# A new order for all engines in the last five rows of an attention and adapter kernel

## The chip, the core and the metric

The kernel runs on one core of a Trainium2 chip. The metric is the time of one execution in device microseconds. Three runs of the kernel before gave 99.35, 99.8 and 100.41 us; the median is 99.8 us. One more execution was profiled, and its trace is what is read below.

## What is computed

Eight batches ("rows" in the kernel, r = 0 to 7) of eight heads, 576 positions, head size 64. Heads 0 to 3 attend to the last 32 positions; heads 4 to 7 to every fourth of the last 128, so that after sorting the positions into four classes they are windowed attention too. Then every token goes through a router over eight small adapters.

```python
scores = scale * np.matmul(q, k.transpose(0, 1, 3, 2))
mask_plain = (rel >= 0) & (rel < window)
mask_dil = (rel >= 0) & (rel < window * dilation) & (rel % dilation == 0)
attn = softmax(where(mask, scores, -1e9));  x = attn @ v     # per head, then heads side by side
...
logits = x @ w_gate                          # 8 adapters, the best two are kept
z = x[mask] @ A[e]                           # 512 -> 16
delta[mask] += w[mask, k, None] * (z @ B[e]) # 16 -> 512, weighted by a softmax over the two
return x + delta
```

## The kernel before

One row's inputs are 3.5 MB of f32, which the loads turn into bf16 on their way into one of four input slots; one row's output is 1.2 MB of f32. Each row has two groups of four heads, g = 0 (plain) and g = 1 (dilated). The work of a row is a list of named steps, and each name is a letter, a row and a group or part:

- `L` loads, issued by POOL (lines 282, 314, 325). Row 4's are `L4a`, `L4b` (queries and keys of the two groups) and `Lw4` (values); rows 5 and 6 likewise. Row 7's are eight pieces, `Lq7..` for queries and keys and `Lv7..` for values. POOL runs them in its own order between its other work, and one waits at the head of POOL's queue until what it depends on is done.
- `S0rg`, `S1rg`: scores of the first five and the last four key blocks on PE, 24 and 20 matmuls (line 222, names `con,one` or `one` for the mask and `in` for the scores). `E0rg`, `E1rg`: their exponentials on ACT (line 370).
- `Vrg`: values, 26 matmuls (`in,p`). `Rrg`, `Nrg`: reciprocal and normalisation on DVE (lines 406, 409).
- `Brg`: cast to bf16 on POOL (line 416). `Trg`, `Ur`: 8 and 2 transposes on PE (lines 433, 457). `Crg`, `Cdr`, `Cpr`: their copies out of PSUM on ACT (lines 443, 446, 463, 467); in row 7 `Bx7` (ACT, line 418), `C71` (ACT, line 449) and `Cx7` (DVE, line 450) take a part.
- `Z0r`, `Z1r`: logits and adapter inputs, 20 matmuls (`aw,xt`); `Y0r`, `Y1r` their copies (ACT, line 491). `m0`, `m1`, `s12`, `top`, `tt`, `g2` on DVE and `th` on ACT (lines 503 to 513): the two best logits and their weights. `gzr`: the weighted adapter inputs on POOL (line 518; on DVE in row 7, as `gz7` and `gy7`).
- `Gr` (and `H7`): 5 transposes (line 523); `gcr`, `gnr` their copies on ACT (lines 539, 542). `Dr0` to `Dr2`: the adapters' outputs on PE (`bt,gc` or `bt,gn`). `Ar0` to `Ar2`: they are added to the row, on DVE (lines 570, 600) or, for parts of rows 4 to 7, by an ACT copy (`dx`, `dy`; lines 596, 576) and a POOL addition (lines 598, 578).
- `Or`: stores, issued by SP (lines 611, 615). Rows 0 to 4 are stored whole, at most two of these in flight; rows 5 to 7 in two halves. All stores wait for row 7's queries and keys to land (`late`).

Nothing schedules at run time. A text, `PLAN`, gives one order of all steps; each engine runs its own steps in that order, and what a step needs from another engine becomes a semaphore wait. A number behind `@` is the first PSUM bank of eight that a step's result gets; the step then also waits until all users of what stood in these banks before are done. So the order and the banks decide together who waits for whom. The text is all that differs between the two kernels.

Of the kernel before, what the change touches and what calls it, by code (L numbers as in the profile page):

```python
# [628 lines left out]
A00 S121@6 E121 S120@3 S021@1 Z01@0 E021 Z11@5 Y01 m01 Y11 m11 s121  # L629
S020@1 D02@0 V21@5 E120 top1 tt1 th1 g21 E020 A02 V20@0 R21 N21 R20 L4a  # L630
gz1 L4b G1@5 gn1 S130@6 N20 gc1 B21 E130 S031@3 D12@2 E031 S030@0 D10@5
T21@7 E030 C21 A12 S131@3 B20 Lw4 V30@0 L5a A10 E131 U2@7 T20@6 R30 N30
Cp2 B30 L5b V31@3 Cd2 C20 Z02@7 Y02 Z12@1 R31 N31 B31 T30@2 D11@6 Y12
C30 S041@4 A11 E041 S141@2 Lw5 S140@6 m02 E141 S040@0 m12 s122 tt2 U3@5
Cp3 th2 E040 top2 Cd3 g22 gz2 L6a V41@2 T31@0 E140 C31 V40@5 R41 N41
Z03@2 G2@0 Y03 gn2 Z13@1 L6b gc2 R40 Y13 N40 B40 Lw6 S051@2 D20@4 E051
A20 m13 S151@6 E151 S050@0 S150@2 E150 m03 s123 V51@5 top3 tt3 T40@3 th3
E050 C40 B41 g23 T41@4 C41 R51 V50@0 N51 R50 D22@5 N50 U4@7 gz3 Lq710
Lq711 Cd4 Cp4 G3@6 gn3 D21@3 gc3 A22 A21 Z04@7 Y04 B50 Lq700 Lq701
S060@0 D32@2 Z14@7 S161@5 m04 E060 Y14 m14 E161 s124 S160@0 A32 T50@7  # L640
E160 D30@3 S061@5 top4 V60@0 A30 tt4 R60 C50 E061 B51 Lv710 Lv711 Lv700
Lv701 O1 T51@3 N60 C51 V61@4 th4 g24 R61 N61 U5@7 S171@2 Cp5 Cd5 S070@0
Z05@7 E171 E070 Z15@6 Y05 S170@2 S071@4 Y15 m05 m15 top5 B60 gz4 E170
E071 s125 G4@0 B61 D31@6 tt5 th5 gn4 V70@1 T60@4 A31 gc4 V71@5 U6@0 C60
O0 g25 O2 gz5 G5@4 Cp6 Cd6 R70 N70 B70 T61@2 D41@0 D42@3 R71 N71 gn5 A41
C61 dx4 gc5 B71 Bx7 D40@5 Z06@2 Y06 Z16@4 Y16 A40 m06 A42 D52@3 m16 s126
dx5 top6 U7@7 Cp7 Cd7 tt6 T71@1 Cx7 C71 T70@4 D51@5 A52 th6 g26 A51
D50@0 A50 C70 gz6 Z07@2 Z17 m07 m17 s127 tt7 dy5 G6@5 gc6 O3 D61@0 th7
gn6 D62@7 A53 top7 O4 O51 O50 dx6 g27 D60@5 gy7 gz7 A62 dy6 A61 A63 O61
G7@3 H7 gm7 gn7 gc7 D72@0 dx7 A72 D71@1 A60 D73@6 O60 A71 D70@7 O71 A70  # L650
dy7 A73 O70
"""

_INS = ["qkv", "aw", "bt", "con"]
# [64 lines left out]
```

## Time and profile before

| | |
|---|---|
| median of three runs | 99.8 us (99.35 to 100.41) |
| the profiled execution | 100.24 us, of which the trace spans 98.5 us |
| granted TensorE clock | 0.983 (0.80 in the last stretch, from 90 us on, where PE has little to do) |
| busy: PE matmuls, ACT, DVE, POOL | 80.6, 71.1, 61.3, 55.5 us |
| loads on POOL's DMA queue | 14.23 MB, as they land |
| stores on SP's DMA queue and three small loads | 9.77 MB |

Times in the trace count from the first instruction. The span ends with the landing of the last store; 1.74 us of the profiled execution lie outside of it. A line of a step that a helper records shows the helper's line (222 for nearly all of PE), so steps are told apart by their operands and their place in the order.

### The profile page before, as it was taken

Reading aid. Unit: us, or ns where it says so; the run is one execution under the profiler, and the core shown is the slowest. Engines: PE = TensorE matmul, PEld = TensorE weight load, DVE = VectorE, ACT = ScalarE, POOL = GpSimd, SP = SyncE. Lnnn points to the kernel's source line nnn. Section 1 sums busy time; section 2 is a strip of 40 time slices with the busy share of each in tenths; the row PEclk is TensorE's granted clock in tenths of the full one; section 3 lists DMA queues with packets and bytes.
Section 4 is the critical chain, followed back from the end, with each engine's and each line's share of the span. In section 5 each row is a group of like instructions: output and inputs, shape, how many; then the busy total and the mean of one; then the engine's idle time right before and its main releaser. Section 6 shows DMA issues by size and latency. Waiting matters only on the chain.

```text
span 98.5 us, 3614 instructions
## 1 busy us (share of the span) xinstructions
PE 80.6 (82%) x1585; PEld 59.6 (60%) x1585; DVE 61.3 (62%) x138; ACT 71.1 (72%) x123; POOL 55.5 (56%) x76
## 2 busy tenths in 40 slices
PE   3999969959569989899899989997995989776500
PEld 2443457548356767689677768885883878564300
DVE  5770007706467179559737667976854999979810
ACT  5294494399938983996986889999596889957400
POOL 5999900810544058826574499397292464665820
PEclk9999999999999999999999999999999999999985
DMA  1999999999999999999999999999999999996894
GB/s 42 305 193 194 199 218 216 213 214 214 212 213 213 212 212 210 217 206 201 208 213 212 216 210 212 199 214 203 194 320 412 400 412 423 396 378 268 354 421 185
DMA packets 5999, 24.50 MB, mean 249 GB/s; under 512 B 864, under 2 KB 992, under 8 KB 5344
## 3 DMA queue, kind: packets, MB, share of 16 engines
q0 software_dynamic: 3968, 14.23, 73.2%
q1 hardware_dynamic: 1872, 9.77, 24.3%
q10 hardware_dynamic: 144, 0.28, 0.8%
q8 instruction: 12, 0.20, 0.7%
q14 instruction: 3, 0.02, 0.1%
HBM read 29.07 MB, written 9.44 MB: 391 GB/s over the span
## 4 chain that ended last, share of the span: by engine, by line
PE 56%; ACT 22%; DVE 9%; issue 4%; POOL 3%; POOLq 0%
PE ps L222 49%; ACT p L370 12%; PE ps L433 5%; DVE x L570 4%; DVE x L409 3%; ACT xt L443 2%; ACT gn L542 2%; PE ps L523 2%; ACT zs L491 1%; POOL x L578 1%; ACT gc L539 1%; ACT in L272 1%; POOL xb L416 1%; PE ps L457 1%; ACT xt L446 1%
## 5 line engine op out<-in xcount | busy, mean ns | idle before, releaser
L370 ACT ACTIVATE p<-ps 128x960 bf16<-128x960 f32 (+1 forms) x32 | 27.7, 902 | 4.3 <-PE ps L222 4.2
L416 POOL CAST xb<-x 128x1152 bf16<-128x1152 f32 (+1 forms) x16 | 18.2, 1139 | 16.9 <-DVE x L409 16.8
L222 PE MATMUL ps<-in,p 128*64 128x130 bf16 (+1 forms) x416 | 21.5, 221 | 3.9 <-ACT p L370 3.1
L409 DVE TENSOR_TENSOR x<-ps,rec 128x1152 f32<-128x1152 f32 x16 | 21.7, 1358 | 0.5
L222 PEld LDWEIGHTS ps<-in,p 128*64 128x64 bf16 (+1 forms) x416 | 17.1, 104 | 7.4 <-ACT p L370 4.2
L570 DVE TENSOR_TENSOR x<-x,ps 128x1024 f32<-128x1024 f32 (+1 forms) x16 | 17.5, 1117 | 4.6 <-PE ps L222 4.6
L406 DVE RECIPROCAL rec<-ps 128x18 f32<-128x18 f32 x16 | 4.3, 270 | 17.3 <-PE ps L222 17.1
L222 PEld LDWEIGHTS ps<-in 64*64 64x64 bf16 x576 | 10.8, 106 | 3.7 <-issue 1.9
L222 PE MATMUL ps<-in 64*64 64x96 bf16 (+1 forms) x576 | 11.8, 201 | 1.5 <-issue 1.5
L222 PE MATMUL ps<-warm 128*128 128x512 f32 x20 | 11.8, 737 | 1.5 <-DVE warm L226 1.5
L518 POOL TENSOR_TENSOR gz<-zs,g 128x640 bf16<-128x640 f32 x7 | 8.9, 1274 | 6.3 <-DVE g L513 6.3
L282 POOL DMA_DIRECT2D in<-in_qkv_dram x22 | 11.6, 572 | 1.4 <-POOLq L702 0.8
L222 PE MATMUL ps<-aw,xt 128*128 128x136 bf16 x160 | 11.2, 223 | 0.1
L443 ACT COPY xt<-ps 128x1024 bf16<-128x1024 bf16 x8 | 8.1, 1011 | 3.7 <-PE ps L433 3.6
L314 POOL DMA_DIRECT2D in<-in_qkv_dram x8 | 5.2, 648 | 9.2 <-PE ps L222 7.3
L222 PEld LDWEIGHTS ps<-aw,xt 128*128 128x128 bf16 x160 | 9.6, 98 | 0.9 <-ACT xt L443 0.4
L433 PE MATMUL ps<-one,xb 128*128 128x128 bf16 x128 | 9.6, 219 | 0.1
L222 PE MATMUL ps<-bt,gn 128*128 128x256 bf16 (+1 forms) x48 | 6.8, 263 | 2.0 <-ACT gn L542 0.8
L433 PEld LDWEIGHTS ps<-one,xb 128*128 128x128 bf16 x128 | 7.5, 98 | 1.5 <-POOL xb L416 0.7
L222 PEld LDWEIGHTS ps<-warm 128*128 128x128 f32 x20 | 4.5, 238 | 6.4 <-issue 4.9
L446 ACT COPY xt<-ps 128x1024 bf16<-128x1024 bf16 x7 | 7.3, 1038 | 1.0 <-PE ps L433 1.0
L222 PE MATMUL ps<-bt,gc 128*128 128x256 bf16 (+1 forms) x48 | 6.6, 255 | 1.5 <-ACT gc L539 1.5
(55 smaller groups left out, 102.4 us busy)
## 6 DMA issues: line engine op xcount, KB each, us to landing
out_dram<-x SPq DMA_DIRECT2D x5, 1152.0 KB, 5.7
in<-in_qkv_dram POOLq DMA_DIRECT2D x6, 576.0 KB, 7.6
out_dram<-x SPq DMA_DIRECT2D x6, 576.0 KB, 3.2
in<-in_qkv_dram POOLq DMA_DIRECT2D x10, 292.5 KB, 7.6
in<-in_qkv_dram POOLq DMA_DIRECT2D x10, 288.0 KB, 6.6
in<-in_qkv_dram POOLq DMA_DIRECT2D x2, 1152.0 KB, 23.3
in<-in_qkv_dram POOLq DMA_DIRECT2D x10, 146.2 KB, 8.0
in<-in_qkv_dram POOLq DMA_DIRECT2D x2, 434.2 KB, 13.8
```

The costliest lines, as they stand in the source:

```text
L222: return nc.tensor.matmul(o, lhsT=lhsT, rhs=rhs, start=start, stop=stop, skip_group_check=True)
L282: nc.gpsimd.dma_start(out=IN[r % SLOTS][half(a), at : at + n], in_=qkv[r, a, :, at - 2 * VB * a : at - 2 * VB * a + n],)
L314: return lambda: [nc.gpsimd.dma_start(out=IN[r % SLOTS][:, 2 * VB + QK * n : 2 * VB + QK * (n + m)].rearrange("p (j n) -> p j n", j=m), in ...
L370: return [nc.scalar.activation(p[:, :, :].rearrange("p h (s c) -> p h s c", c=PER)[:, :, b0 : b0 + nb, 0:SEG], PS[:, k.at : k.at + 2, 0 : ...
L406: rc = add(f"R{tag}", "DVE", ("el", 60), lambda: [nc.vector.reciprocal(rec[:, :].rearrange("p (b i) -> p b i", b=3), PS[:, k.at : k.at + 3 ...
L409: nm = add(f"N{tag}", "DVE", ("el", XG), lambda: [nc.vector.tensor_tensor(X[r][:, XG * g : XG * g + XG].rearrange("p (b i n) -> p b i n", ...
L416: add(f"B{tag}", "POOL", ("el", cut), lambda: [nc.gpsimd.tensor_copy(XB[r % 2][:, g, 0:cut], X[r][:, XG * g : XG * g + cut])], [nm] + free)
L433: nc.tensor.transpose(tp[j][:, 128 * u : 128 * u + 128], xb[:, g, 256 * u + 128 * j : 256 * u + 128 * j + 128], ident())
L443: return [nc.scalar.copy(xt[:, 0:2, 0:S].rearrange("p j (c i) -> p j c i", c=C)[:, :, :, 0:128], tp.rearrange("p j (i c) -> p j c i", c=C))]
L446: return [nc.scalar.copy(xt[:, 2:4, 0:512], tp)]
L518: return [en.tensor_tensor(GZ[i][:, us[0] : us[0] + n, :].rearrange("p u (e r) -> p u e r", e=E), zv()[:, us[0] : us[0] + n, 0:ER].rearran ...
L570: return [nc.vector.tensor_tensor(v, v, PS[:, k.at : k.at + nk].rearrange("p b n -> p (b n)"), ALU.add)]
```

## The change

The second half of `PLAN` is replaced, from `V30`'s successors to the end; the steps, their instructions, their sizes and their data are the same, and so is the first half of the order. All engines' orders and the bank numbers change in rows 3 to 7. The loads keep their order among themselves; the step names between which they stand change. A line or two of the text:

```diff
-T21@7 E030 C21 A12 S131@3 B20 Lw4 V30@0 L5a A10 E131 U2@7 T20@6 R30 N30
-Cp2 B30 L5b V31@3 Cd2 C20 Z02@7 Y02 Z12@1 R31 N31 B31 T30@2 D11@6 Y12
...
+T21@7 E030 C21 A12 S131@3 B20 Lw4 V30@0 E131 A10 U2@6 R30 N30 Cp2 L5a
+Cd2 T20@7 C20 V31@3 Z12@6 Y12 S041@1 Z02@0 B30 T30@6 L5b R31 N31 D11@4
...
```

Three places show what this does. On PE, around the values of row 5 (`in1,p3` is group 1, `in1,p2` group 0; `in2` is row 6's slot). Before:

```order
L222 MATMUL ps<-in1,p3 64x130 x18
L222 MATMUL ps<-in1,p3 128x130 x8
L433 MATMUL ps<-one,xb0 128x128 x16
L222 MATMUL ps<-in1,p2 64x130 x18
L222 MATMUL ps<-in1,p2 128x130 x8
L222 MATMUL ps<-bt,gn0 64x128 x2
L222 MATMUL ps<-bt,gc0 64x128 x2
L457 MATMUL ps<-one,xb0 128x128 x2
```

And in the changed kernel, at the same place:

```order
L222 MATMUL ps<-in1,p3 64x130 x18
L222 MATMUL ps<-in1,p3 128x130 x8
L222 MATMUL ps<-one 64x384 x4
L222 MATMUL ps<-in2 64x96 x12
L222 MATMUL ps<-in2 64x64 x4
L433 MATMUL ps<-one,xb0 128x128 x16
L222 MATMUL ps<-in1,p2 64x130 x18
L222 MATMUL ps<-in1,p2 128x130 x8
L457 MATMUL ps<-one,xb0 128x128 x2
```

Row 6's first scores, `S160`, now stand behind `V51` and ahead of `T41`, `T40` and `V50`; they stood behind `S161`, some 120 matmuls later. `D22`, the four small matmuls ahead of `U4`, moved up to row 5's scores. On ACT `E160` moved with `S160`, ahead of `C41` and `C40`.

On PE, ahead of the values of row 7's group 0 (`in3,p2`). Before:

```order
L222 MATMUL ps<-aw,xt1 128x136 x20
L222 MATMUL ps<-one 64x384 x4
L222 MATMUL ps<-in3 64x96 x12
L222 MATMUL ps<-in3 64x64 x4
L222 MATMUL ps<-con,one 64x480 x4
L222 MATMUL ps<-in3 64x96 x20
L523 MATMUL ps<-one,gz0 128x128 x5
L222 MATMUL ps<-bt,gc1 128x256 x4
L222 MATMUL ps<-in3,p2 64x130 x18
```

In the changed kernel:

```order
L222 MATMUL ps<-one 64x480 x4
L222 MATMUL ps<-in3 64x96 x20
L222 MATMUL ps<-bt,gn1 64x128 x2
L222 MATMUL ps<-bt,gc1 64x128 x2
L222 MATMUL ps<-bt,gc1 128x256 x4
L523 MATMUL ps<-one,gz0 128x128 x5
L222 MATMUL ps<-con,one 64x480 x4
L222 MATMUL ps<-in3 64x96 x20
L222 MATMUL ps<-in3,p2 64x130 x18
```

`S071` (the last `con,one` and `in3` rows) stood ahead of `G4` and `D31`; now `D32`, `D31` and `G4` stand ahead of it. `V70` has 1389 matmuls ahead of it in both orders.

On ACT, in the tail: the copies of row 6's logits (line 491), of row 7's transposes (467, 463, 449, 443), `th6` (510) and the copy `dx5` (596). Before:

```order
L491 COPY zs0<-ps 128x408
L491 COPY zs0<-ps 128x272
L596 COPY awf<-ps 128x256
L467 COPY xt1<-ps 128x2x64
L463 COPY xt1<-ps 128x2x4x16
L449 COPY xt1<-ps 128x512
L510 ACTIVATE th0<-tt0 128x40
L443 COPY xt1<-ps 128x2x4x128
L576 COPY in0<-ps 128x512
```

In the changed kernel:

```order
L491 COPY zs0<-ps 128x408
L491 COPY zs0<-ps 128x272
L463 COPY xt1<-ps 128x2x4x16
L467 COPY xt1<-ps 128x2x64
L449 COPY xt1<-ps 128x512
L510 ACTIVATE th0<-tt0 128x40
L443 COPY xt1<-ps 128x2x4x128
L596 COPY awf<-ps 128x256
L576 COPY in0<-ps 128x512
```

`dx5` moved from ahead of row 7's copies to behind them. Its matmuls `D52` moved in the same way on PE (from ahead of `U7` to behind `D51`), and its addition `A52` on POOL from ahead of `gz6` to behind it. From `D61` on, PE's order is the old one.

More of the change, by code (lines that the diff above doesn't have):

```diff
@@ L631 @@
 gz1 L4b G1@5 gn1 S130@6 N20 gc1 B21 E130 S031@3 D12@2 E031 S030@0 D10@5
-T21@7 E030 C21 A12 S131@3 B20 Lw4 V30@0 L5a A10 E131 U2@7 T20@6 R30 N30
-Cp2 B30 L5b V31@3 Cd2 C20 Z02@7 Y02 Z12@1 R31 N31 B31 T30@2 D11@6 Y12
[L634 to L651, printed above, removed]
+T21@7 E030 C21 A12 S131@3 B20 Lw4 V30@0 E131 A10 U2@6 R30 N30 Cp2 L5a
@@ new lines @@
+Cd2 T20@7 C20 V31@3 Z12@6 Y12 S041@1 Z02@0 B30 T30@6 L5b R31 N31 D11@4
+E041 Y02 m12 S141@2 S040@0 A11 C30 E141 B31 S140@6 U3@5 V41@2 E040 m02
+s122 top2 tt2 th2 T31@1 g22 R41 Cd3 Lw5 N41 E140 Cp3 V40@5 R40 C31 N40
+gz2 G2@4 Z03@0 gn2 S051@1 gc2 L6a Y03 Z13@3 D20@4 E051 Y13 A20 D22@0 A22
+m13 B41 S151@6 E151 m03 L6b B40 S050@1 S150@3 E050 top3 s123 tt3 th3 Lw6
+V51@5 R51 g23 S160@0 E150 E160 gz3 T41@4 C41 T40@3 Lq710 C40 N51 V50@0
+U4@6 R50 N50 D21@4 A21 G3@7 Cp4 Cd4 gc3 gn3 Z04@6 S061@2 Z14@7 S060@0
@@ new lines @@
+Y04 E061 S161@4 Y14 E060 m04 m14 Lq711 E161 B50 T50@3 D30@6 Lq700 Lq701
+O2 V60@0 s124 A30 top4 R60 B51 U5@4 C50 Cp5 Lv710 T51@7 Cd5 V61@4 N60
+S171@0 Lv711 tt4 C51 Lv700 th4 R61 E171 Z05@2 Lv701 Y05 g24 N61 Z15@7
+Y15 m15 m05 S170@0 B60 S070@2 gz4 D32@4 E170 s125 A32 tt5 D31@6 E070
+top5 th5 G4@0 S071@4 E071 V70@1 g25 gz5 gn4 B61 T60@4 gc4 A31 R70 N70
+V71@5 C60 U6@0 R71 O1 Cd6 Cp6 G5@2 T61@4 D41@0 gc5 N71 C61 D42@3 gn5 dx4
+B70 A41 D40@6 Z06@4 A40 Bx7 Y06 Z16@0 Y16 m06 m16 B71 U7@5 s126 A42
+T71@1 T70@4 O0 top6 Cd7 Cp7 C71 tt6 th6 C70 D51@6 O3 Cx7 D52@5 dx5 D50@0
@@ L652 @@
+g26 A51 dy5 A50 Z07@2 Z17 gz6 G6@6 gc6 m07 O4 m17 s127 tt7 th7 top7 g27
+gz7 gy7 D61@0 gn6 D62@7 A52 A53 dx6 A62 D60@5 dy6 O51 A61 A63 G7@2 H7
+O50 gc7 gn7 gm7 O61 D72@0 A60 O60 D71@1 D73@4 D70@3 A71 dx7 A72 A70 dy7
+O71 A73 O70
 """
```

## Prediction

> **What bounds the kernel now.** I read the page first, for the DMA row and the queues.
>
> ```profile
> span 98.5 us, 3614 instructions
> DMA  1999999999999999999999999999999999996894
> q0 software_dynamic: 3968, 14.23, 73.2%
> q1 hardware_dynamic: 1872, 9.77, 24.3%
> q8 instruction: 12, 0.20, 0.7%
> ```
>
> The DMA engines are busy nearly throughout: loads (q0) take 73.2% of 16 engines' span, stores and small loads (q1) 24.3%. Together that is 97.5% of 98.5 us, 96.0 us. The kernel has little room whatever its order. To see where that room is, I read the busy time by windows in the store phase (us, five engines, clock, DMA share, GB/s).
>
> ```profile
> 86.00:90.00 4.00, 3.22 (x44) 2.56 (x45) 3.44 (x14) 2.24 (x6) 2.01 (x3) 1.00 0.91 377
> 90.00:92.00 2.00, 1.19 (x17) 0.89 (x15) 1.64 (x3) 1.49 (x4) 1.81 (x3) 1.00 0.40 164
> 92.00:96.00 4.00, 0.47 (x5) 0.18 (x2) 1.82 (x2) 0.58 (x1) 1.98 (x2) 0.89 1.02 422
> ```
>
> The room is a hole between 90 and 92 us, 0.60 x 2 = 1.2 us, and 0.09 x 4 = 0.36 us ahead of it. The stores had run dry; `O61` (row 6, group 1) was waiting for `A61` on DVE. From 92 us on the last four half stores run back to back at 422 GB/s. So **the end is set by when `A61` is done**, and up to 1.6 us are to be had.
>
> Then I read the chain of waits, in order of time (start, us, what), from 57 us on.
>
> ```profile
> 57.15 0.47 issue
> 68.39 0.58 issue
> 74.05 1.04 issue
> 79.65 1.36 DVE x L409
> 84.99 0.91 ACT xt L443
> ```
>
> PE carries it until 79 us, with three holes called "issue", time in which PE waited for nothing that the profile shows. I took the queue table over 0.03 us windows from 55.17, 66.67 and 72.71 us, and the matmuls between the stalls' ends.
>
> ```profile
> q8 instruction: 1, 0.02, 195.0%
> q8 instruction: 1, 0.02, 203.1%
> q8 instruction: 1, 0.02, 200.2%
> ...
> 57.61:68.96 11.35, 10.77 (x253) 1.00 1.06 208
> 68.96:75.08 6.12, 5.06 (x126) 1.00 1.05 284
> ```
>
> Each window holds the start of one instruction fetch. The stalls end at 57.62, 68.97 and 75.09 us, 2.44, 2.29 and 2.37 us behind those starts, and they are 253 = 2 x 126.5 and 126 matmuls apart. So PE's instructions come in blocks of some 126.5 matmuls; counting `PLAN`, the stalled ones are matmuls 981, 1234 and 1360, with 1107 between. A block costs 5.68 us (11.35 / 2) to 6.12 us however it is ordered, although PE's own work in it is less: from 68.97 to 75.09, 5.06 of 6.12 us. **Until 75 us PE is paced by the fetch of its instructions**, and order only decides what stands in a block.
>
> The Trainium skill (Runtime: NRT & Kernel Launch, Instruction fetch mechanics) says that the next 16 KiB block of 256 instructions is fetched while the current one runs and that crossing is "mostly hidden". The block size agrees with 2 x 126.5 instructions; hidden it is not here, with 0.47, 0.58 and 1.04 us.
>
> **The change part by part.** Nothing is added: same steps, same bytes, same instruction count, so the load time and the number of fetches stay.
>
> *Blocks up to 1360.* `S160` now heads PE's queue behind `V51`, and needs row 6's first load, `L6a`.
>
> ```profile
> 52.17 0.60 POOL L314 DMA_DIRECT2D in<-in_qkv_dram  x1
> ...
> DMA to landing us min/median/max: 7.5/7.5/7.5
> 58.10 1.34 PE L222 MATMUL ps<-in,p 128*64 128x130 bf16 x26
> 58.29 0.81 ACT L370 ACTIVATE p<-ps 128x768 bf16<-128x768 f32 x1 [0.35 <-PE ps L222]
> 84.89 0.99 ACT L443 COPY xt<-ps 128x1024 bf16<-128x1024 bf16 x1
> 62.09 0.27 ACT L463 COPY xt<-ps 128x128 bf16<-128x128 bf16 x1 [0.19 <-PE ps L457]
> 63.65 0.41 PE L222 MATMUL ps<-in 64*64 64x96 bf16 x20
> ```
>
> `L6a` is issued at 52.17 and lands 7.5 us later, at 59.67; loads queue behind one another, so it keeps that time. `V51` ended at 59.44 before. So PE stands 0.2 to 0.5 us, with `T41`, `T40` and `V50` queued behind. Then: `S160` about 0.5, `E160` 0.81, two copies of 0.99 as `C70` took (`C41`, `C40`; ACT starts one about 0.1 ahead of the last one's end, as `C70` behind `th6` at 84.75 + 0.24), `Cp4`, `Cd4` 0.27 each with the same overlap. 59.67 + 0.5 + 0.1 + 0.81 + 0.89 + 0.89 + 0.17 + 0.17 = 63.2, and `Z04` starts at 63.2 to 63.4, with PE's wait for each hand-over. `Z04` is matmuls 1106 to 1117, so matmul 1107 is passed by 63.4; before, it was `S060`, in the row at 63.65. That is 0.25 to 0.3 earlier, and the two blocks behind it cost what they cost: 1360 at about 74.8 instead of 75.09. Bounds: two blocks at 5.68 each give 74.8, two at 6.12 give 75.6.
>
> ```profile
> 60.27 0.31 PE L222 MATMUL ps<-in,p 128*64 128x130 bf16 x4
> 61.34 0.53 POOL L282 DMA_DIRECT2D in<-in_qkv_dram  x1
> 64.45 0.51 POOL L282 DMA_DIRECT2D in<-in_qkv_dram  x1
> ...
> DMA to landing us min/median/max: 6.2/6.6/7.0
> ```
>
> `V50` needs `E160`'s banks and comes some 0.9 later (59.67 + 0.5 + 0.1 + 0.81 = 61.1, for 60.27), so `N50`, `B50` and the two loads behind `B50` on POOL (`Lq700`, `Lq701`) too, 65.35 for 64.45. The piece ahead of them, issued at 61.34, lands at most 7.0 us later, at 68.3, so 3 us of DMA work cover them; if not, each us of delay is a us of idle DMA, of which the hole of 1.2 us takes up the first.
>
> *From 1360 to `V70`.*
>
> ```profile
> 75.09 0.41 PE L222 MATMUL ps<-in 64*64 64x96 bf16 x20 [1.04 <-issue]
> 75.43 0.45 PE L523 MATMUL ps<-one,gz 128*128 128x128 bf16 x5
> 76.25 1.33 PE L222 MATMUL ps<-in,p 128*64 128x130 bf16 x26
> 68.16 1.04 POOL L282 DMA_DIRECT2D in<-in_qkv_dram  x2 [0.57 <-ACT xt L443]
> ...
> DMA to landing us min/median/max: 5.1/5.6/6.1
> ```
>
> Before, 20 matmuls of `S071`, `G4` and `D31` lay between: 1.16 us. Now `G4` (75.43 to 75.72, 0.28) and all of `S071` (0.41 for its 20 scores, the row at 75.09, and an estimated 0.15 for the four masks ahead of them): 0.84. So `V70` starts at 74.8 + 0.84 = 75.65 to 75.95, 0.3 to 0.6 earlier; I take 0.45. What is late next is its values, `Lv701`, the second of the pair at 68.16, so issued near 68.7 and landing 6.1 us later, at 74.8: no `V70` before that, so at most 1.45 are gained here.
>
> *The tail.* `V70`, `T60`, `V71`, `R71`, `N71`, `A41`, `A40` stand as before and move with `V70`. Behind them:
>
> ```profile
> 83.29 0.46 ACT L596 COPY awf<-ps 128x256 f32<-128x256 f32 x1
> 83.83 0.73 POOL L598 TENSOR_TENSOR x<-x,awf 128x256 f32<-128x256 f32 x1 [1.40 <-ACT awf L596]
> 83.86 0.75 DVE L511 TENSOR_TENSOR top<-zs,mx 128x40 f32<-128x40 f32 x1
> ...
> 88.01 0.19 DVE L511 TENSOR_TENSOR top<-ps,mx 128x40 f32<-128x40 f32 x1
> 83.92 0.65 ACT L449 COPY xt<-ps 128x512 bf16<-128x512 bf16 x1
> 84.75 0.24 ACT L510 ACTIVATE th<-tt 128x40 f32<-128x40 f32 x1 [0.17 <-DVE tt L508]
> ```
>
> `top6` took 0.75 us beside `A52` on POOL, and 0.19 elsewhere (`top7`). `A52` now follows `gz6`, so `tt6` is ready 0.56 earlier. With `D52` (0.23 of PE) out from ahead of `U7`, `T71` and so `C71` come 0.23 earlier, at 83.7, and end at 84.35; `th6`, 84.75 before, follows at 84.25 (ACT's overlap), and `C70` behind it at 84.4 instead of 84.89. That is 0.5. `gz6`, 1.3 us from some 0.4 behind `th6`, then ends near 86.1, ahead of `G6`, which PE reaches 2 us behind `C70`'s end of 85.4. `dx5`, `A52`, `A53` end by 87.8 as before, off the path. I take 0.45 for the tail; between 0 (something else, such as `Bx7`, holds `C70`) and 0.56.
>
> The Trainium skill (SBUF — State Buffer, SBUF: two separate sides) has a rule for the 0.75: a VectorE operation with two SBUF inputs and a GpSimd operation that reads SBUF lock each other out for a whole instruction. The rows agree: 83.86 + 0.75 ends right behind 83.83 + 0.73.
>
> Sum: 0.45 + 0.45 = 0.9 us, all ahead of `A61`, and within the 1.6 us that the stores can take up. Against the profiled execution 100.24 - 0.9 = 99.3; that execution lay 0.44 above the median, so against the median 99.8 - 0.9 = **98.9 us**.
>
> **The rivals.**
>
> *The fetch lets go.* If the new order passes matmuls 855 and 981 earlier as well, or crossings are hidden, as that page of the Trainium skill would have it, PE is no longer held at 1360. Then `V70` waits for `Lv701` at 74.8, 1.45 gained, with the tail 1.9, of which the DMA can take up 1.6: 98.2 us. For it: PE work of 5.06 in a block of 6.12. Against it: three measured stalls and the load that `S160` waits for. 17%.
>
> *The wait at `S160` decides (slower).* PE's place is behind `V51`, the cause the landing of `L6a`. If it lands 1 us late (7.5 becomes 8.5), or `gz2` ahead of it on POOL is late by that, `Z04` and matmul 1107 pass at 64.4, and two blocks at 6.12 put 1360 at 76.6, 1.5 late; `V70` is then 1.2 late, with the tail's 0.45 the end 0.75 late: 100.5 us; without the tail's gain 101.0. It decides from 63.7 on, where 1107 passed before. For it: that the load has no slack, 59.67 against 59.44. Against it: loads queue in one row at an even rate. 18%.
>
> *The change moves the order and not the end.* Two blocks at 6.12 (1360 at 75.6) eat `V70`'s gain, and `C70` is held by another wait: 99.8 us. 15%.
>
> **How the numbers follow.** Forecast 50%, its own range 98.5 to 99.5 (0.3 to 1.3 gained). About 1% is what a measurement of this kernel can tell from no change. Faster by more than that is under 98.8: the first rival and nearly half of the forecast, 0.17 + 0.23 = 0.40. Slower is over 100.8: half of the second rival, 0.09, and 0.01 for what I have not seen: 0.10. The rest, 0.50, is within 1%. The range takes in the floor (98.2, with 0.2 for the spread of runs) and most of the slower case: 98.0 to 100.4.
>
> **What would show it.** Right: a PE stall called issue that ends at 74.5 to 75.2 with `G4` behind it; `V70` at 75.6 to 76.0; `top6` at 0.19 us; `C70` at 83.9 to 84.1; `O61` issued near 89.8, and a DMA share in the 2 us behind 90 well over 0.40. Wrong: `S160` later than 60.2, a load row with idle DMA between 66 and 72 us, or a `C70` that waits for something other than `th6`.

## The result, and the profile after

The changed kernel takes **101.67 us**, the median of six runs (100.96 to 103.74). The kernel before takes 100.27 us, also over six runs (99.35 to 100.86; the three from above and three more). The ratio is **1.014 with a 95% interval of 1.0097 to 1.0182**: slower, where the prediction had 98.9 us and a range up to 100.4. (In this and all comparisons below a run over 1.5% above the fastest of its kernel is left out of the ratio, so a ratio can differ a little from that of the medians.) The profiled execution took 101.5 us, 1.26 us more than the one before.

First the rows of the page that answer to those quoted of before: span, DMA share in 40 slices, GB/s in the same slices, and the two large queues.

```profile
span 99.7 us, 3612 instructions
DMA  2999999999999999999999989999999999989993
GB/s 32 307 205 207 209 215 221 205 212 214 216 216 207 220 210 214 209 210 198 200 216 213 209 142 192 191 202 180 182 229 414 414 413 414 387 368 375 401 420 137
q0 software_dynamic: 3968, 14.23, 73.2%
q1 hardware_dynamic: 1872, 9.77, 24.1%
```

The DMA row is as full as before, and the two queues still fill 97.3% of the span. What is new stands in the GB/s row: from the 24th slice to the 29th (57 to 72 us) the loads move 142 to 202 GB/s. Here are these microseconds by window, first of the kernel before, then of the changed one (us, then PE, PEld, DVE, ACT, POOL, clock, DMA share, GB/s).

```profile
56.00:60.00 4.00, 3.52 (x106) 2.88 (x105) 2.66 (x12) 3.65 (x8) 3.78 (x6) 1.00 1.04 205
60.00:66.00 6.00, 6.00 (x142) 4.89 (x140) 4.96 (x12) 5.63 (x11) 4.50 (x7) 1.00 1.05 207
66.00:72.00 6.00, 5.40 (x140) 4.26 (x138) 4.66 (x9) 4.57 (x9) 3.60 (x6) 1.00 1.06 204
72.00:74.00 2.00, 2.00 (x48) 1.53 (x44) 0.85 (x4) 2.00 (x5) 2.00 (x3) 1.00 1.10 353
```

```profile
56.00:60.00 4.00, 3.42 (x101) 2.65 (x100) 2.48 (x11) 3.31 (x7) 2.66 (x4) 1.00 0.92 163
60.00:66.00 6.00, 5.81 (x120) 4.74 (x119) 4.33 (x6) 5.41 (x10) 3.29 (x4) 1.00 1.02 192
66.00:72.00 6.00, 5.08 (x119) 4.01 (x117) 3.70 (x12) 4.98 (x8) 4.96 (x9) 1.00 1.02 187
72.00:74.00 2.00, 2.00 (x46) 1.79 (x47) 1.40 (x3) 1.19 (x4) 1.47 (x2) 1.00 1.06 180
```

At 72 us the kernel before was storing already (353 GB/s are mostly stores); the changed one was still loading. Its share reads 0.92 to 1.06 all the while, so the share alone hides the loss, and only beside GB/s is it seen. The requests that belong to this, on POOL (start, us, line; with what POOL waited for ahead of one):

```profile
52.15 0.60 POOL L314 DMA_DIRECT2D in<-in_qkv_dram  x1
56.81 0.54 POOL L314 DMA_DIRECT2D in<-in_qkv_dram  x1 [2.73 <-PE ps L222]
58.43 1.04 POOL L325 DMA_DIRECT2D in<-in_qkv_dram  x2
62.16 1.09 POOL L282 DMA_DIRECT2D in<-in_qkv_dram  x2
66.12 1.03 POOL L282 DMA_DIRECT2D in<-in_qkv_dram  x2
68.22 1.04 POOL L282 DMA_DIRECT2D in<-in_qkv_dram  x2
70.03 1.04 POOL L282 DMA_DIRECT2D in<-in_qkv_dram  x2 [0.78 <-ACT xt L443]
```

These are `L6a`, `L6b`, `Lw6` and the four pairs of row 7. In the kernel before the same rows read:

```profile
52.17 0.60 POOL L314 DMA_DIRECT2D in<-in_qkv_dram  x1
55.51 0.53 POOL L314 DMA_DIRECT2D in<-in_qkv_dram  x1 [2.74 <-PE ps L222]
57.12 1.04 POOL L325 DMA_DIRECT2D in<-in_qkv_dram  x2
60.77 1.09 POOL L282 DMA_DIRECT2D in<-in_qkv_dram  x2
64.45 1.02 POOL L282 DMA_DIRECT2D in<-in_qkv_dram  x2
66.55 1.03 POOL L282 DMA_DIRECT2D in<-in_qkv_dram  x2
68.16 1.04 POOL L282 DMA_DIRECT2D in<-in_qkv_dram  x2 [0.57 <-ACT xt L443]
```

So `L6a` keeps its time, and **all that follow are requested 1.30 to 1.87 us later**. `Lq701` lands at 72.48 instead of 71.10, the first store is issued at 72.62 instead of 71.16, and the last load packet ends at 76.00 instead of 73.95.

The store phase, against the hole shown of before:

```profile
86.00:90.00 4.00, 3.11 (x41) 2.24 (x39) 3.44 (x13) 2.83 (x6) 3.19 (x3) 1.00 0.95 397
90.00:92.00 2.00, 1.25 (x18) 0.91 (x14) 2.00 (x5) 1.63 (x4) 1.33 (x2) 1.00 0.94 385
92.00:96.00 4.00, 1.28 (x12) 0.86 (x12) 2.33 (x3) 0.96 (x2) 2.66 (x3) 1.00 0.95 392
```

The hole at 90 us (share 0.40) is gone, 0.94 now. It is not gone because the work came earlier: `O61` is issued at 91.58, 0.88 later than before. The stores began 1.46 us later and had that much more of a backlog.

PE was late too. The chain of waits names more and longer holes called issue, and the rows around `V70` (26 matmuls, `in,p`) stand later:

```profile
45.90 0.34 issue
51.28 1.36 issue
57.99 0.58 issue
64.33 0.19 issue
69.63 0.84 issue
...
85.77 1.00 ACT xt L443
```

```profile
76.69 0.44 PE L523 MATMUL ps<-one,gz 128*128 128x128 bf16 x5 [0.75 <-ACT th L510]
77.06 0.40 PE L222 MATMUL ps<-con,one 64*64 64x480 bf16 x4
77.29 0.38 PE L222 MATMUL ps<-in 64*64 64x96 bf16 x20
77.60 1.33 PE L222 MATMUL ps<-in,p 128*64 128x130 bf16 x26
```

`V70` starts at 77.60 instead of 76.25. `C70` (the row at 85.77) is 0.88 later than before, and so is `A61`, at 90.34. Two things therefore stand side by side, loads that end late and PE that runs late, and either could be the cause of the other or of the time.

### The profile page after: what moved, and what is told of

It reads as the page before. It is cut to its first block, busy times and chain, and to the rows that moved or that the text cites. A ratio compares the mean times of both kernels' runs of the same rounds, so it can differ in the third digit from the quotient of the medians.

```text
span 99.7 us, 3612 instructions
## 1 busy us (share of the span) xinstructions
PE 80.3 (81%) x1585; PEld 59.5 (60%) x1585; DVE 60.1 (60%) x138; ACT 71.0 (71%) x123; POOL 55.6 (56%) x76
## 4 chain that ended last, share of the span: by engine, by line
PE 56%; ACT 27%; issue 5%; DVE 4%; POOL 3%; POOLq 0%
PE ps L222 48%; ACT p L370 12%; PE ps L433 5%; ACT gn L542 2%; ACT zs L491 2%; ACT xt L443 2%; ACT xt L446 2%; PE ps L523 2%; ACT gc L539 2%; DVE x L409 1%; POOL x L578 1%; DVE x L570 1%; PE ps L457 1%; ACT in L272 1%; POOL xb L416 1%
## 5 line engine op out<-in xcount | busy, mean ns | idle before, releaser
L222 PE MATMUL ps<-warm 128*128 128x512 f32 x20 | 11.3, 712 | 1.5 <-DVE warm L226 1.5
(55 smaller groups left out, 101.5 us busy)
## 6 DMA issues: line engine op xcount, KB each, us to landing
in<-in_qkv_dram POOLq DMA_DIRECT2D x2, 1152.0 KB, 22.7
```

Of the source, the lines that this page charges most:

```text
L222: return nc.tensor.matmul(o, lhsT=lhsT, rhs=rhs, start=start, stop=stop, skip_group_check=True)
```

## The experiments

**The theories.** *Loads*: the requests from `L6b` on come too late for the DMA queue, the loads end late, and the end follows them whatever PE does. *Fetch*: PE's blocks of code are fetched at worse moments (the 1.36 us at 51.28), PE runs late, and that sets the end; the loads are late only because POOL waits for PE. *Tail*: the new tail costs time instead of gaining it. A fourth stands in the expectations of 3 and 4, *S160*: the new place of `S160` delays `V50`, `B50` and so `Lq700`, which would make it the origin of late requests.

**1. The changed order with its requests made early.** In the changed kernel each load from `L6b` on moves one to three POOL steps up, and the holds behind `Z13` and `C50` go. PE, ACT and DVE keep the changed order.

```diff
-    6: (None, "Z13", None),
-    7: (None, None, None, "C50"),
+    6: (None, None, None),
+    7: (None, None, None, None),
...
-gz2 G2@4 Z03@0 gn2 S051@1 gc2 L6a Y03 Z13@3 D20@4 E051 Y13 A20 D22@0 A22
+gz2 G2@4 Z03@0 gn2 S051@1 gc2 L6a L6b Y03 Z13@3 D20@4 E051 Y13 A20 D22@0
```

> The changed kernel with its loads from L6b on issued one to three POOL steps earlier (L6b right behind L6a, Lw6 ahead of B40, Lq710 and Lq711 ahead of gz3, Lq700 to Lv711 ahead of B50, Lv700 and Lv701 ahead of B51) and without the holds behind Z13 and C50; all other engines' orders stay. Load theory (late requests let the loads end 2 us late, and the stores with them): loads end near 74 us, the first store is issued near 71.2, and the time falls by the 1.2 to 1.4 us that the change lost, to a ratio of 1.00 to the kernel before. Fetch theory (PE's stalls for instruction blocks moved V70 from 76.25 to 77.60, and A61 with it): V70 stays within 0.4 us of 77.6 and O61 near 91.6; the stores only win what they waited beyond that, 0.3 to 0.4 us, ratio 1.010.

Measured: ratio 0.9995 (0.9949 to 1.004), so the whole loss is gone. Its windows:

```profile
56.00:60.00 4.00, 3.17 (x96) 2.33 (x94) 2.44 (x11) 3.16 (x6) 1.84 (x3) 1.00 1.05 214
60.00:66.00 6.00, 5.05 (x109) 4.24 (x109) 3.87 (x6) 4.61 (x9) 3.94 (x6) 1.00 1.06 213
66.00:72.00 6.00, 5.89 (x141) 4.68 (x134) 4.10 (x12) 5.51 (x10) 3.12 (x5) 1.00 1.06 208
72.00:74.00 2.00, 2.00 (x60) 1.75 (x64) 1.97 (x3) 1.43 (x3) 1.86 (x2) 1.00 0.95 287
```

The loads move 208 to 214 GB/s, and the last packet ends at 74.49. PE gained as well (`V70` 76.32, `A61` 89.06), so this run speaks for the loads but does not exclude the fetch.

**2. The old order with the new tail alone.** `D52` moves behind `D51`, `dx5` behind `C70`, `A52` behind `gz6`; nothing ahead of the tail changes.

```diff
-dx5 top6 U7@7 Cp7 Cd7 tt6 T71@1 Cx7 C71 T70@4 D51@5 A52 th6 g26 A51
-D50@0 A50 C70 gz6 Z07@2 Z17 m07 m17 s127 tt7 dy5 G6@5 gc6 O3 D61@0 th7
+U7@7 Cp7 Cd7 tt6 T71@1 Cx7 C71 T70@4 D51@5 D52@7 th6 g26 A51 D50@0 A50
+C70 dx5 gz6 A52 Z07@2 Z17 m07 m17 s127 tt7 dy5 G6@5 gc6 O3 D61@0 th7 gn6
```

> The kernel before, with only the tail's moves: dx5 behind C70, D52 behind D51 (bank 7), A52 behind gz6, gz7 ahead of gy7, gn7 ahead of gm7. Fetch theory: V70 stays near 76.25, the 0.47 to 0.54 us that the changed kernel's tail won between V70 and Z07 reach O61, 90.2 instead of 90.7, and the end: ratio 0.995. Load theory (the stores' start sets the end): the hole in the stores at 90 to 92 us would not be there to fill, ratio 1.000.

Measured: 0.9946 (0.99 to 0.9992), 100.14 us beside 100.52. `top6` takes 0.19 us, and from `A40` to `C70` it is 2.49 us instead of 2.84. The tail theory falls: the tail gains about half a microsecond, and in the old order this reaches the end. It is the only version whose interval lies below 1, by little.

**3. The old order up to `V51`, the changed one behind it.**

```diff
-A20 m13 S151@6 E151 S050@0 S150@2 E150 m03 s123 V51@5 top3 tt3 T40@3 th3
-E050 C40 B41 g23 T41@4 C41 R51 V50@0 N51 R50 D22@5 N50 U4@7 gz3 Lq710
...
+A20 m13 S151@6 E151 S050@0 S150@2 E150 m03 s123 V51@5 B41 E050 D22@0 A22
+top3 tt3 th3 R51 g23 S160@0 E160 gz3 T41@4 C41 T40@3 Lq710 C40 N51 V50@0
...
```

> The old order up to V51, the new one behind it (S160 right behind V51, the new tail), A22, B41 and D22 at the seam. Fetch theory: the time was lost at the block that begins at matmul 855, in T31, ahead of the seam; so this one has V70 at 75.9 to 76.6 and, with the tail's 0.5, a ratio of 0.993 to 1.000. S160 theory (the place of S160 holds PE and delays V50, B50 and Lq700): as slow as the changed kernel, 1.010 to 1.015.

Measured: 1.0154 (1.0102 to 1.0205), as slow as the whole change. Here the two theories part, because PE is *not* late: `V70` starts at 76.27 (before: 76.25), `A61` at 89.01, 0.45 earlier than before. Yet the last store lands at 99.13, 1.51 later. Two load windows and the store phase:

```profile
60.00:66.00 6.00, 5.44 (x115) 4.64 (x116) 4.81 (x9) 4.95 (x10) 3.29 (x4) 1.00 1.01 189
66.00:72.00 6.00, 5.60 (x136) 4.46 (x136) 3.86 (x13) 5.14 (x9) 5.11 (x9) 1.00 0.99 178
...
86.00:90.00 4.00, 3.14 (x42) 2.31 (x39) 3.44 (x13) 2.47 (x7) 2.69 (x4) 1.00 1.00 414
90.00:92.00 2.00, 1.26 (x12) 0.86 (x12) 1.56 (x4) 1.20 (x4) 1.80 (x3) 1.00 1.01 415
```

The loads lost their rate between 60 and 72 us, and from 84 us on the stores ran without a hole, at 414 GB/s from 86 us: at the end no store was waiting for PE or DVE. The 1.51 us are not all the loads', though. In this execution the 16 DMA engines do not finish together: their share is 1.05 from 96.0 to 96.5 us and then 0.83, 0.25, 0.13 and 0.09 in the half microseconds up to 98.5. In the kernel before it is 0.98 up to 97.0 and 0.24 up to 97.5, where it ends. Spread evenly over the engines, the last store packets would have ended at 97.3 in both (an estimate from the packets' times). So here the late loads used up the hole, and what is left of the 1.51 us is a few engines that lag behind the others. Whether these are the engines on which the loads had been slow is not shown; the records do not name a packet's engine.

**4. The changed order up to `V51`, the old one behind it.**

```diff
-V51@5 R51 g23 S160@0 E150 E160 gz3 T41@4 C41 T40@3 Lq710 C40 N51 V50@0
...
+V51@5 E150 T40@3 C40 g23 T41@4 C41 R51 V50@0 N51 R50 N50 U4@7 gz3 Lq710
+Lq711 Cd4 Cp4 G3@6 gn3 D21@3 gc3 A21 Z04@7 Y04 B50 Lq700 Lq701 S060@0
...
```

> The new order up to V51, the old one behind it. Fetch theory: the stall of 1.36 us at matmul 855 is there again, V51 starts near 59.1 instead of 58.1, and the old rest carries that to the end without the tail's 0.5: ratio 1.010 to 1.018. S160 theory: 1.000.

Measured: 1.0041 (1.0 to 1.0082). The fetch theory had put this run at the full loss, and misses. The hole at block 855, 1.58 us from one weight load's start to the next in the changed kernel, was 0.73 us here, in the same order: its size differs from execution to execution.

The third and the fourth together show where the late requests come from. In the third `S160` starts at 60.42, as in the changed kernel, though something else holds it there: it waits for DVE, where `A22`, which reads its bank, ends at 60.28 and `top3`, the step that the profile names, at 60.39; in the changed kernel it stands behind `V51`. `E160` follows, `V50` comes at 61.93 in both (60.27 before), and `Lq700`, behind `V50`, `N50` and `B50`, is requested at 66.11 and 66.12. In the fourth, with `S160` back in its old place, `V50` starts at 60.43 and `Lq700` is requested at 64.61, 0.16 later than before. So row 7's last three pairs are late because `V50` now waits for `E160`, which follows `S160`, as the S160 theory has it; it had put the two runs at 1.010 to 1.015 and at 1.000. `L6b` is another matter. It is on time in the third (55.24), and in the fourth, with the hole at 0.73 us, only 0.20 later than before (55.71). Its 1.30 us in the changed kernel thus go with the hole at 51.28 in that execution.

**5. The old order with late requests.** PE, ACT, DVE and SP keep the order of before word for word. Only POOL's order and holds change: `L6b` behind `S151` and `B41`, `Lq710` and `Lq711` behind `G3`, `Lq700` and `Lq701` behind `T50`. The cast `B41` thereby moves ahead of `B40`.

```diff
-    6: (None, "Z13", None),
-    7: (None, None, None, "C50"),
+    6: (None, "S151", None),
+    7: ("T50", "G3", None, "C50"),
```

> The kernel before with its loads from L6b on requested about as late as the changed kernel does: L6b held behind S151 (56.8 us), Lq710 and Lq711 behind G3 (62.4), Lq700 and Lq701 behind T50 (66.3), the others behind these on POOL; PE, ACT, DVE and SP keep the old order word for word. Load theory: the load rate falls from some 210 to 150-190 GB/s between 57 and 73 us, Lq701 lands near 72.5 instead of 71.1, the stores run without a hole to the end, ratio 1.010 to 1.016. Fetch theory: V70 within 0.5 us of 76.25 and the ratio 0.998 to 1.004.

Measured: 1.018 (1.0109 to 1.025), 102.19 us beside 100.75. The suspected cause, put into the old order, costs all that the change cost. PE was later as well (`V70` 76.87, 0.62 later than before), but the fourth is the control for that: there `V70` is at 76.86 and `A61` at 90.08, here 76.87 and 90.09, and with requests at most 0.2 us behind those of before its ratio is 1.0041. The load theory had expected stores without a hole; the share from 90 to 92 us is 0.78.

```profile
56.00:60.00 4.00, 3.43 (x106) 2.91 (x102) 3.55 (x12) 3.56 (x7) 3.21 (x5) 1.00 0.94 160
60.00:66.00 6.00, 5.76 (x135) 4.65 (x134) 4.53 (x12) 5.20 (x10) 2.98 (x4) 1.00 1.03 191
66.00:72.00 6.00, 4.57 (x98) 3.65 (x95) 4.21 (x8) 4.06 (x6) 4.17 (x7) 1.00 0.99 179
72.00:74.00 2.00, 1.60 (x54) 1.29 (x53) 1.68 (x3) 1.50 (x4) 1.96 (x2) 1.00 1.06 187
```

These four rows are nearly those of the changed kernel: 160, 191, 179, 187 GB/s against 163, 192, 187, 180.

**6. The old order, the new tail and early requests.** Experiment 2, with the requests moved up and the holds removed as in experiment 1.

```diff
-Cp3 th2 E040 top2 Cd3 g22 gz2 L6a V41@2 T31@0 E140 C31 V40@5 R41 N41
+Cp3 th2 E040 top2 Cd3 g22 gz2 L6a L6b Lw6 V41@2 T31@0 E140 C31 V40@5 R41
...
+E050 C40 B41 g23 T41@4 C41 R51 V50@0 N51 R50 D22@5 N50 U4@7 Lq710 Lq711
+gz3 Lq700 Lq701 Lv710 Lv711 Cd4 Cp4 G3@6 gn3 D21@3 gc3 A22 A21 Z04@7 Y04
...
```

> The kernel before with the new tail (as in the run with the new tail alone) and its loads from L6b on requested one to three POOL steps earlier, without the holds behind Z13 and C50. Load theory: loads at 210 GB/s throughout end 0.3 to 0.6 us earlier than 74.75, Lq701 lands at 70.5 to 70.8; the end is then set by A61 again, ratio 0.990 to 0.996. Fetch theory: as with the new tail alone, 0.9946.

Measured: 1.0027 (0.9984 to 1.0071), medians 100.47 and 100.75. Its profiled execution is the shortest of those that do the whole work (99.33 us, last store landing at 96.70), but the runs do not bear out a gain, and the expectation misses. The load phase is full (214 GB/s from 54 to 60 us, 212 from 60 to 66), and holes open in the stores instead (share 0.81 from 86 to 92 us): with the loads early, the compute comes last again, as in the kernel before.

**7. Experiment 6 with PE's blocks shifted.** 64 more PE instructions stand at the start, so that the borders of the blocks of 126.5 matmuls fall 64 matmuls earlier in the program.

```diff
-            mm(bank(k), w, w[:, 0:1].to_broadcast([128, 512]), True, True) for _ in range(n)][:0], after, k)
+            mm(bank(k), w, w[:, 0:1].to_broadcast([128, 512]), True, True) for _ in range(n)] + [
+            mm(bank(k)[:, 0:1], WARM[:, 0:128], WARM[:, 0:1], True, True) for _ in range(pads)])[:0], after, k)
...
-    scratch("warm", 5, ["wz"], 1.05)
+    scratch("warm", 2, ["wz"], 1.05)
```

> The run before this one (early loads, new tail) with 64 more matmul instructions ahead of the first scores: three of the five wide warming matmuls, two instructions each, give way to 70 matmuls of one column. So every block of PE instructions ends about 64 matmuls earlier in the list of steps, half a block, and V70 stands at the end of a block, not at the start of the next. Fetch theory: V70 comes 0.5 to 1.4 us earlier than in the run before this one (at most until Lv701 has landed, 74.6), and the end 0.3 to 1.0 us earlier, ratio 0.983 to 0.992. Load theory: no change from the run before this one, 0.990 to 0.996.

Measured: 1.0514 (1.0437 to 1.0591). The run is flawed: the short matmuls replaced long ones of the warm-up, and the granted clock was 0.87 from 12 to 16 us and 0.71 from 16 to 20, where the sixth had 1.00. How much the borders cost cannot be told from it, so it was mended as experiment 11.

**8. The changed order with light loads.** The loads of rows 4 to 6 bring a quarter of their columns, so the DMA engines have little to do from 40 to 62 us.

```diff
-                out=IN[r % SLOTS][half(h), ROW * h : ROW * h + 2 * VB],
+                out=IN[r % SLOTS][half(h), ROW * h : ROW * h + (2 * VB if r < 4 else VB // 2)],
```

> The changed kernel, with the loads of rows 4 to 6 bringing only a quarter of their columns; the rest of these slots keeps the data of rows 0 to 3, so the output of rows 4 to 6 is not the reference's. DMA engines are mostly idle from 43 to 60 us. If the fetch of PE's instructions waits for busy DMA engines, a block of 126.5 matmuls takes 4.8 to 5.2 us there instead of 5.9 to 6.0, and the stalls at matmuls 855 and 981 go. If the fetch has a fixed latency, the stalls stay at 0.6 to 1.4 us and the blocks at 5.9.

Measured, one execution: 99.21 us. The fetch of the next block starts 0.41 to 1.10 us behind the matmuls that open blocks 602, 728 and 855; in the changed kernel it starts 3.57 to 4.59 us behind those that open 728, 855 and 981. The holes at 855 and 981 are gone. So the fetch's lateness comes from busy DMA engines and is not a fixed latency. PE then ran far ahead (`V70` 73.43, 4.17 earlier than in the changed kernel, `A61` 86.14), and the last store landed only 2.28 earlier, at 96.58: the end follows the last load packet, at 72.95, by 23.6 us. (Here too the DMA engines end unevenly: their share is 0.27 from 94.5 to 95.0 us and falls to 0.02 at the end.)

**9 and 10. The late requests by halves.** In the changed order, once only `L6b` and `Lw6` are requested early (row 7 stays late), once only row 7's pieces (row 6 stays late).

```diff
-gz2 G2@4 Z03@0 gn2 S051@1 gc2 L6a Y03 Z13@3 D20@4 E051 Y13 A20 D22@0 A22
-m13 B41 S151@6 E151 m03 L6b B40 S050@1 S150@3 E050 top3 s123 tt3 th3 Lw6
+gz2 G2@4 Z03@0 gn2 S051@1 gc2 L6a L6b Y03 Z13@3 D20@4 E051 Y13 A20 D22@0
+A22 m13 B41 S151@6 E151 m03 Lw6 B40 S050@1 S150@3 E050 top3 s123 tt3 th3
```

> The changed kernel's order, with only the loads of row 6 requested early (L6b, which loses its hold behind Z13, near 53 us, Lw6 near 55 us); the requests of row 7 stay where the change put them (Lq711 near 62.7, Lq701 near 66.6). It asks which of the late requests costs the time. If what is lost between 56 and 60 us decides: those windows go back to 205 to 215 GB/s, the later loads follow without loss, ratio 0.997 to 1.003. If each late request costs its own share: 56 to 60 us is full, a window between 66 and 74 us falls under 185 GB/s, Lq701 lands near 72.0 to 72.4 and the ratio is 1.004 to 1.012. If fetches of PE's code decide, nothing changes against the changed kernel: 1.010 to 1.018.

```diff
-V51@5 R51 g23 S160@0 E150 E160 gz3 T41@4 C41 T40@3 Lq710 C40 N51 V50@0
...
+Lq710 Lq711 V51@5 R51 g23 S160@0 E150 E160 gz3 Lq700 Lq701 Lv710 Lv711
+T41@4 C41 T40@3 C40 N51 V50@0 U4@6 R50 N50 D21@4 A21 G3@7 Cp4 Cd4 gc3
...
```

> The other half: the changed kernel's order with L6b and Lw6 as late as the change has them (near 56.8 and 58.4 us), and the six requests of row 7 one to three POOL steps earlier (Lq711 near 60, Lv701 near 67 us). If each late request costs its own share: the windows from 56 to 60 us stay under 185 GB/s (some 0.2 MB less than at 210 GB/s, which is 0.9 us), from 62 us on they are at 200 or more, Lq701 lands near 72.0 to 72.5 and the ratio is 1.004 to 1.012. If the row 7 requests are what costs: ratio 0.997 to 1.003. If fetches of PE's code decide: 1.010 to 1.018.

Measured: 1.0105 (1.0022 to 1.0189) with row 6 early, 0.9975 (0.9915 to 1.0035; medians 100.97 and 100.79) with row 7 early. The window in which each loses rate, first of experiment 9, then of 10:

```profile
66.00:68.00 2.00, 2.00 (x58) 1.58 (x44) 1.00 (x4) 2.00 (x5) 2.00 (x4) 1.00 1.00 163
```

```profile
58.00:60.00 2.00, 1.86 (x50) 1.54 (x54) 1.18 (x10) 1.97 (x4) 2.00 (x5) 1.00 0.90 164
66.00:68.00 2.00, 2.00 (x60) 1.47 (x57) 0.40 (x3) 2.00 (x4) 1.81 (x3) 1.00 1.05 212
```

Each late group loses rate at its own place, as expected. Row 7's four late pairs cost most of the time; row 6's two alone cost nothing that can be measured, although PE is still late in the tenth (`V70` 77.07, `A61` 89.81). (The ninth's profiled execution, 100.7 us, was the fastest of its four, so its load end in the table below is a favourable one.) The reading that each late request costs a share by itself misses in the ratio of the tenth run.

**11. Experiment 7 mended.** The short matmuls stand ahead of the long ones; the clock is 1.00 from 12 to 20 us and 0.90 from 20 to 24.

```diff
-            mm(bank(k), w, w[:, 0:1].to_broadcast([128, 512]), True, True) for _ in range(n)][:0], after, k)
+            mm(bank(k)[:, 0:1], WARM[:, 0:128], WARM[:, 0:1], True, True) for _ in range(pads)] + [
+            mm(bank(k), w, w[:, 0:1].to_broadcast([128, 512]), True, True) for _ in range(n)])[:0], after, k)
...
-    scratch("warm", 5, ["wz"], 1.05)
+    scratch("warm", 3, ["wz"], 1.05)
```

> The run with shifted blocks again, with its flaw mended: the kernel of the sixth experiment (old order, early loads, new tail) with 64 more PE instructions at the start, this time with the long warm-up matmuls behind the short ones, so that the granted clock should stay at 1.00 between 12 and 20 us (it was 0.87 and 0.71 in the seventh). Everything from the first load on is the same code, only the borders of PE's blocks of 126.5 instructions lie 64 matmuls earlier in the program. If the place of the borders does not matter: 0.992 to 1.006 and A61 near 88 to 90. If it does: stalls of over 1.2 us at borders again (the seventh run had them at 45.9, 64.2, 76.8 and 83.0), V70 and A61 over 2 us later than in the sixth (75.55 and 88.43), ratio over 1.015. A clock under 0.9 between 12 and 20 us makes the run useless once more.

Measured: 1.0423 (1.0316 to 1.0531). The 64 short matmuls at the start make the program 4.2% slower, though everything behind them is the code of the sixth. The chain of waits has these holes (the profiled execution, 106.61 us, was this kernel's slowest of four, so the rows are read for their places):

```profile
45.16 1.02 issue
63.07 1.39 issue
82.81 0.47 issue
```

From one weight load's start to the next there are gaps of 1.23, 1.66, 0.76 and 1.98 us, ending at 46.18, 64.46, 76.45 and 83.25. The last store landed 26.7 us behind the last load packet, where all others but the seventh lie near 23, and the stores had a hole from 86 to 90 us (share 0.40). So here the compute set the end. `A61` is 6.0 us later than in the sixth run and the four gaps explain 5.6 at most, some of which the sixth had too (1.70 at one border). What the rest is stays open, and so does whether the borders alone make the gaps.

## What decided the time

Three numbers of each profiled execution (us; the last packet of the loads is taken from the DMA records):

| kernel | `A61` | last load packet ends | last store lands | from load end to end |
|---|---|---|---|---|
| before | 89.46 | 73.95 | 97.62 | 23.67 |
| changed | 90.34 | 76.00 | 98.86 | 22.86 |
| 1, changed order, early requests | 89.06 | 74.49 | 97.41 | 22.92 |
| 2, old order, new tail | 88.71 | 74.16 | 97.27 | 23.11 |
| 3, old head, new rest | 89.01 | 75.34 | 99.13 | 23.79 |
| 4, new head, old rest | 90.08 | 74.73 | 98.24 | 23.51 |
| 5, old order, late requests | 90.09 | 75.90 | 98.83 | 22.93 |
| 6, old order, early, new tail | 88.43 | 73.19 | 96.70 | 23.51 |
| 8, light loads | 86.14 | 72.95 | 96.58 | 23.63 |
| 9, row 6 early | 87.95 | 74.75 | 98.08 | 23.33 |
| 10, row 7 early | 89.81 | 74.57 | 97.97 | 23.40 |
| 11, shifted blocks | 94.45 | 77.16 | 103.89 | 26.73 |

In all but the last row the end lies 22.9 to 23.8 us behind the end of the loads, while `A61` ranges over 4.2 us. (Experiment 7, which is left out, is like 11: 27.2 us.) The store packets alone take 22.7 to 22.8 us of each engine, as a mean over 16; what holes, uneven engines and the overlap with the last loads add or save stays within 0.9. That the ends agree across orders, and even with light loads, is why I call the loads the cause. A filled hole is not a pure gain: in 3, 8 and 9, where the stores have none, the engines end unevenly as described under 3. In the changed kernel only 0.3 of the 1.24 us are of that kind.

Why a late request slows the loads shows in the DMA's packet records. A load packet of 4608 bytes takes 0.361 us at the median in both kernels. From 46 us to the end of the loads I split the time into that of all load packets at the median of their size (over 16 engines), what packets took beyond it, and the rest. The rest is a balance: it holds time in which engines had no packet, 0.36 to 0.39 us of packets of 4 bytes and the first stores, less what packets overlap, so only its differences are read:

| kernel | time | at the median | stretched packets | rest |
|---|---|---|---|---|
| before | 27.95 | 27.03 | 0.53 | 0.39 |
| changed | 30.00 | 26.67 | 1.77 | 1.57 |
| 1 | 28.49 | 27.60 | 0.07 | 0.81 |
| 3 | 29.34 | 26.73 | 1.42 | 1.18 |
| 5 | 29.90 | 26.67 | 1.98 | 1.26 |
| 6 | 27.19 | 26.55 | 0.15 | 0.49 |
| 9 | 28.75 | 26.76 | 1.22 | 0.77 |
| 10 | 28.57 | 27.49 | 0.52 | 0.56 |

The bytes cost the same; what grew are the stretched packets (52 of them over 0.55 us from 46 us on, 11 before) and the rest, by 1.18 us, 0.93 of it ahead of the first store packet. The stretched ones stand in clusters around the moments at which the queue comes to a late load: at 58.0 to 58.7 us packets of 0.8 to 1.0 us, where `L6b`, issued at 56.81, begins. From issue to a load's first packet it is 1.4 us there, 2.3 (`Lq710`) and 1.8 (`Lq700`); before it was 2.55, 2.5 and 2.3, and there one packet of 1.92 us at 58.1 and a few stretched ones at 63.3 and 68.1 stand already. In experiment 1 it was 6.8 for `Lq710`, with one stretched packet in all. (Which load a packet belongs to I took from its size and its place in the row.) Counted the same way over the traces of before, of the changed kernel and of experiments 1 to 6, 9 and 10, from `L6a` on: the 9 loads with a lead of 1.9 us or less have 5 to 13 stretched packets each; of 79 with 2.2 to 5.1 us 37 have some, 10 at most; of 32 with over 5.1 us none has any. So **a request that comes less than 2 us ahead of its first packet goes with a slow start of its load every time, one that comes over 5 us ahead never**, and there is no sharp edge between. That the queue has run dry by then is the reading of this; the lowest lead of all, 1.27 us, would be what a request needs at an empty queue. Why such packets take two to three times as long is not shown; the records have no more.

The Trainium skill (DMA: Bandwidth & Descriptors, Latency and other measured facts) gives about 1 us to the first byte of a transfer issued by GpSimd. The 1.4 us of `L6b` is near it, so a request has to be made at least that much ahead.

## Why the prediction was wrong, by its own steps

- **What bounds the kernel.** It read that both queues fill 97.5% of the span and that there is little room; that holds. It then placed the room in the hole at 90 us and made `A61` the end's cause. The hole was filled in the changed kernel, and the end came later all the same.
- **The failed step** is in the block part: "so the load time and the number of fetches stay", and its price, "so 3 us of DMA work cover them". The 3 us were counted from an issue at 65.35 to a landing at 68.3. A landing comes 1.2 us behind the last packet (`Lq711`: packets end at 67.09, landing at 68.33), and a request needs 1.4 us to its first packet. The first packet of `Lq700` was at 66.74 before, its issue at 64.45: the cover was 2.3 - 1.4 = 0.9 us, not 3. The delay was not 0.9 either but 1.67 (66.12 for 64.45), by the path that it had named (`V50` came 1.66 later), and the other requests were late too, which the prediction did not follow: `L6b` 1.30 behind `Z13`, `Lw6` 1.31, `Lq71` 1.39, `Lv71` 1.67, `Lv70` 1.87. Its own fallback, that each microsecond of delay is one of idle DMA, was nearly right: up to 1.87 us of delay, 2.05 us at the end of the loads, of which 1.24 reached the last landing. Experiment 5 shows this step in the old order.
- **`S160` and matmul 1107.** Forecast: `L6a` at 59.67 holds PE for 0.2 to 0.5 us, 1107 passes by 63.4. `L6a` landed at 60.07 and `S160` started at 60.42, but behind `V51`, which was itself 1.05 late from the hole at 51.28; PE did not stand for the load. 1107 passed at 64.51, 1360 at 76.66 instead of 74.8. The blocks cost 5.93 to 6.18 us where 5.68 to 6.12 was assumed. PE's lateness of 1.35 at `V70` is real, but experiments 3, 4 and 10 show that it did not make the time.
- **`V70` 0.45 earlier.** It came 1.35 later; the part between 1360 and `V70` was 0.94 us, where 0.84 was forecast (it was 1.16).
- **The tail's 0.45.** Right. `top6` took 0.19 us, `C70` stood behind `th6` with it as the last wait, and from `V70` to `A61` it is 12.74 us instead of 13.21, 0.47 less. Experiment 2 carries it to the end.
- **The rivals.** "The wait at `S160` decides" had nearly the size (100.5 to 101.0) and the right step, but carried its delay to the end by way of PE and `A61` and not by the requests. None of the rivals was a late request, although POOL's wait of 2.74 us ahead of `L6b` stood in the trace. The DMA share near 1 was taken for a rate that keeps; beside GB/s it is not.

## What to carry to other kernels

Where queues fill the span, ask of every moved step first what it does to the requests: how long ahead of its turn each is made, measured from issue to the first packet and not to the landing. Read the DMA share only beside GB/s, since a queue that keeps running dry can show a share of 1 at 160 to 190 GB/s of 207. A gain on the engines reaches the end only as far as the transfers leave a hole for it. Requests made early cost nothing that could be measured here (ratios 0.9995, 1.0027 and 0.9975 in experiments 1, 6 and 10), and their loads kept their rate.

## What was not expected of the hardware

- Load packets at the start of a late requested load take 0.6 to 1.2 us instead of 0.36, many of them at once.
- When the stores have no hole, the 16 DMA engines can end up to 1.5 us out of step (experiments 3, 8 and 9: an estimate from the share of their last 3 us).
- PE's instruction fetch starts 3.6 to 4.6 us behind the opening of a block while the loads fill the DMA engines, and 0.4 to 1.1 us while they are light (experiment 8); matmuls go on 2.3 to 2.6 us behind the fetch's start when PE stalled for it. The Trainium skill (Runtime: NRT & Kernel Launch, Instruction fetch mechanics) calls the crossing "mostly hidden": with light loads that agrees, under full ones PE stood up to 1.36 us at a border in the changed kernel (the row at 51.28).
- 64 more short PE instructions at the start, under a clock of 1.00 from 12 to 20 us, cost 4.2% (experiment 11). Gaps of 0.76 to 1.98 us at four borders are part of it; the whole was not settled.
